# K's copy moved to VectorE, a third place for raw weight words, and a new planned order: pooled attention with a rational MLP on one Trainium2 core

## The chip, the cores and the metric

The kernel runs on one core of one Trainium2 chip. The metric is the device time of one execution in microseconds (us). The median of three runs before the change is 932.64 us.

## The reference

Pooled attention over 4 batches of 8 heads (1152 keys, 64 wide; pairs of queries are averaged, so 576 queries per head), then an MLP (512 to 2048 to 512) on 2304 tokens whose activation is a rational function.

```python
q_pool = q.reshape(B, H, S // 2, 2, D).mean(axis=3)
scores = 1.0 / np.sqrt(D) * np.matmul(q_pool, k.transpose(0, 1, 3, 2))
attn = np.exp(scores - np.max(scores, axis=-1, keepdims=True))
attn = attn / (np.sum(attn, axis=-1, keepdims=True) + 1e-09)
x = np.matmul(attn, v)          # then heads side by side: 2304 x 512
h = x @ w_in
P = a[0] + a[1] * h + a[2] * h**2 + a[3] * h**3
Q = 1.0 + np.abs(b[0]) * np.abs(h) + np.abs(b[1]) * h**2
out = (P / (Q + 1e-06)) @ w_out
```

## The kernel before

**Numbers.** Every factor of a product is split into a high and a low 16-bit part, so that f16 matmuls give nearly f32 results.

**Attention.** The work is cut into 16 preparations (one for each batch and each pair of heads) and 144 tiles of 128 queries. A preparation loads K, Q and V (SP's queue), takes their ranges (ACT, L608), splits them (ACT L662 to L669, DVE L675 to L684) and transposes K and Q by DMA (L689). A second copy of the upper 64 rows of K, `kb`, lies over a row of ones that was set once (`pr_kb`, L692, a DMA from SBUF to SBUF); with it the scores are computed again with the maximum subtracted in the product. For two head pairs of the last batch the operands are saved and read back later, and `kb` is made anew; that gives 18 copies in all. A tile is a chain: `at_fill` (PE, L720) makes scores in the PSUM tile `sc`, `at_max` (DVE, L727) reduces them, `at_turn` and `at_row` (PE L730, ACT L734) put the maximum into a row of Q, `at_fill2` (PE, L743 and L744, the second one with `kb`) makes scores with the maximum taken off in the PSUM tile `st`, `at_exp` (ACT, L751) takes the exponential and `at_split` (DVE, L759) scales its two halves. `at_pv` (PE, L773) multiplies with V. There is one `sc` and one `st`.

**Weights.** `w_in` and `w_out` arrive in 16 pieces each of 128 x 512 8-byte words into `NRAW=2` raw buffers (`w_load`, L458). Each piece is converted to f32 in the tile `wf` by ACT (`w_win`, L467), POOL (`w_low`, L471, in place) and DVE (`w_bits`, L475), and ACT takes its squares (`w_stat`, L480). When all 16 are there, 8 pairs of `w_hi` (ACT, L502) and `w_lo` (DVE, L506) write the 16-bit weights. `w_in` comes first, then four sums of its magnitudes that use the raw buffers again (L511), then `w_out` through the same buffers. `wf` has one buffer; before, each weight takes it as a tile of its own. When both weights are done, `w_close` gives the space to the MLP's tiles; everything of the MLP but `ch_rcp` (L874) and `ch_norm` waits for that (`late`).

**MLP.** 18 chunks of 128 tokens, each with 4 steps of two products (L915, and L986 to L988) with the activation on ACT, DVE and POOL between them. A chunk starts when its attention tiles are done: the first one needs the first two tiles of the fourth head pair of batch 0.

**Order.** Every engine runs its instructions in the order in which they are written out. That order is made on the host, before the launch, by `Plan`: each operation has an engine, a duration, a due time and the things that it reads and writes; `Plan.forward` schedules by rank, and some rounds back and forth keep the best. A DMA is costed as (issue, transfer, lead). `stirred` perturbs the best order with a random seed and keeps it where the planned end is earlier; before, the list of seeds, `stir`, is empty.

Of the kernel before, what the change touches and what calls it, by code (L numbers as in the profile page):

```python
# [29 lines left out]
    order0=[0, 4, 1, 5, 2, 6, 3, 7, 8], order1=[0, 4, 1, 5, 8, 2, 6, 3, 7], cv=5.63, p_head2=1.05, m0=8.0,  # L30
    stir=[],
    o=14.0, o_last=14.0, c0=2.0, mw=1.2, mf=1.2, ma=1.0, w0=60.0, w1=110.0, ws=2.5, wl=1.44,
# [237 lines left out]
def kernel(  # L270
# [54 lines left out]
    add = plan.add  # L325
    T_COPY, T_TR2 = 450, (625, 3050, 625)

    def cost(n_bytes):
        return (T_COPY, n_bytes / 360.0, T_COPY - 1)

# [115 lines left out]
    def w_open():  # L446
        st["stg_cm"] = tc.tile_pool(name="stg", bufs=1)
        st["stg"] = st["stg_cm"].__enter__()

    def w_load(n, i):  # L450

        t = st["stg"].tile([P, 512, 2], I32, tag="raw", name=f"raw_{n}{i}", bufs=NRAW)
        st["raw", n, i] = t
        if n == "wi":
            src = w_in.bitcast(I32)[i // 4 * P:(i // 4 + 1) * P, (i % 4) * 1024:(i % 4 + 1) * 1024]
        else:
            src = w_out.bitcast(I32)[i * P:(i + 1) * P, :]
        nc.sync.dma_start(out=t.rearrange("p f w -> p (f w)"), in_=src)  # L458
# [4 lines left out]
    def w_win(n, i):  # L463
        if i == 0:
            st["wf", n] = st["stg"].tile([P, 16, 512], F32, tag="wf", name=f"wf_{n}")
        u = st["raw", n, i][:, :, 1].bitcast(F32)
        nc.scalar.activation(out=st["wf", n][:, i, :], in_=u, func=AF.Prelu, scale=2.0 ** -111, alpha=-(2.0 ** 32))  # L467
# [223 lines left out]
    def pr_kb(j):  # L691
        nc.sync.dma_start(out=pr_new(j, "kb")[0:D], in_=pairs[j]["k"][0:D])  # L692

# [103 lines left out]
    def batches(c):  # L797
        return (c // 4,) if c < 4 * B else (2 * (c - 4 * B), 2 * (c - 4 * B) + 1)
# [225 lines left out]
    def prep(j, part):  # L1024
# [8 lines left out]
        if mode == "again":  # L1033
            if hp < 2:
                for i in (0, 1) if part == 0 else (2, 3, 4):
                    add("dma", cost(256 * op_cols(i)), at[6], lambda i=i: pr_again(j, i), r=[("kept", bb, hp, i)], w=[("set", o, i)], seq=["seqag"])
                if part == 0:
                    add("dma", (625, 820, 624), at[7], lambda: pr_kb(j), r=[("set", o, 1)], w=[("set", o, 5)])
            return
        if part == 1:  # L1040
            add("act", 1240, at[14], lambda: pr_hi(j, "v"), r=["vn", ("ss", j)], w=[("set", o, 2)])
            add("dve", 1500, at[15], lambda: pr_lo(j, "v"), r=["vn", ("ss", j), ("set", o, 2)], w=[("set", o, 3)])
            add("dve", 370, at[16], lambda: pr_v3(j), r=[("set", o, 2)], w=[("set", o, 4)])
            if mode == "first" and hp < 2:
                for i in range(5):
                    add("dma", cost(256 * op_cols(i)), at[17], lambda i=i: pr_save(j, i), r=[("set", o, i)], w=[("kept", bb, hp, i)], seq=["seqsv"])
            return
        add("dma", cost(128 * 4608), at[0], lambda: pr_load_k(j), w=["kn"])
        add("dma", (1400, 1640, 449), at[0], lambda: pr_load_q(j), w=["qn"])
        add("dma", cost(128 * 4608), at[1], lambda: pr_load_v(j), w=["vn"])  # L1050
        add("pool", 1500, at[6], lambda: pr_pool(j), w=["qn"])
        add("act", 1146, at[6], lambda: pr_stat(j, 0), r=["kn"], w=[("st", j), "spk"])
        add("act", 700, at[6], lambda: pr_stat(j, 1), r=["qn"], w=[("st", j), "spk"])
        add("act", 1146, at[6], lambda: pr_stat(j, 2), r=["vn"], w=[("st", j), "spk"])
        chain(at[7], half_exp(lambda: pairs[j]["st"]), w=[("st", j)])
# [6 lines left out]
        for i, w in enumerate(("k", "q")):  # L1062
            add("act", 1240, at[8 + 2 * i], lambda w=w: pr_hi(j, w), r=[w + "n", ("ss", j)], w=["sp" + w])
            add("dve", 820 if w == "q" else 1650, at[9 + 2 * i], lambda w=w: pr_lo(j, w), r=[w + "n", ("ss", j)], w=["sp" + w])
            add("dma", T_TR2, at[9 + 2 * i], lambda w=w: pr_tr(j, w), r=["sp" + w], w=[("set", o, 0 if w == "q" else 1)])
            if w == "k":
                add("dma", (625, 820, 624), at[10], lambda: pr_kb(j), r=[("set", o, 1)], w=[("set", o, 5)])

    def attend(t):
        j, slot = tiles[t]  # L1070
        o = j % 2
        s = time_of(t)
        jp = prep_of[j]
        E = ("E", t % NE)
        M = ("M", t % NM)
        wide = slot == 8
        add("pe", (650, 1100) if wide else (490, 960), s, lambda: at_fill(t), r=[("set", o, 0), ("set", o, 1)], w=["S"], seq=["seqS"], bank=B_S)
        add("dve", 1330, s + 0.6, lambda: at_max(t), r=["S"], w=[M], bank=B_S)
        add("pe", (60, 128), s + 2.1, lambda: at_turn(t), r=[M], w=["TURN"], seq=["seqM"], bank=B_TURN)
        add("act", 230, s + 2.3, lambda: at_row(t), r=["TURN", ("set", o, 0)], w=[("row", t)], bank=B_TURN)  # L1080
        add("pe", (1150, 2304) if wide else (1010, 2304), s + 2.7, lambda: at_fill2(t), r=[("row", t), ("set", o, 0), ("set", o, 1), ("set", o, 5)], w=["T"], seq=["seqT"], bank=B_T)
        add("act", 1300, s + 3.9, lambda: at_exp(t), r=["T", ("esc", jp)], w=[E], seq=["seqE"], bank=B_T)
        add("dve", 780, s + 5.3, lambda: at_split(t), w=[E], seq=["seql"])

    def product(g, host):
        j, bb, hp, slot, _ = at_rows(g)
        s = time_of(host) + PRM["pv"]
        V = ("PV", g % 2)
        jp = prep_of[j]
        x = ("x", slot, hp) if slot < 8 else ("x", slot, hp, bb % 2)  # L1090
        add("pe", (1600, 3000), s, lambda: at_pv(g), r=[("set", j % 2, i) for i in (2, 3, 4)] + [("E", t % NE) for t in groups[g]], w=[V], seq=["seqP"], bank=B_PV[g % 2])
        add("act", 370, s + PRM["pvx"], lambda: at_x(g), r=[V], w=[x], seq=["seqx"], bank=B_PV[g % 2])

    def weights(n, s0):
        for i in range(16):
            s = s0 + PRM["ws"] * i
            raw, wf = ("raw", i % NRAW), ("wf", i)
            add("dma", cost(128 * 4096), s, lambda i=i: w_load(n, i), w=[raw], seq=["raw"])
            add("act", 630, s + 4, lambda i=i: w_win(n, i), r=[raw], w=[wf], seq=["win"])
            add("pool", 830, s + 4, lambda i=i: w_low(n, i), w=[(*raw, "low")], r=[raw], seq=["low"])  # L1100
            add("dve", 800, s + 4, lambda i=i: w_bits(n, i), r=[raw, (*raw, "low")], w=[wf])
            add("act", 615, s + 6, lambda i=i: w_stat(n, i), r=[wf], w=[("wst", n, i)])
        s = s0 + 16 * PRM["ws"] + 2
# [4 lines left out]
        for i in range(8):  # L1108
            wf = [("wf", 2 * i), ("wf", 2 * i + 1)]
            add("act", 1141, s + PRM["wl"] * i, lambda i=i: w_hi(n, i), r=wf + [("sw", n)], w=[(n, 0, i)])  # L1110
            add("dve", 1330, s + PRM["wl"] * i, lambda i=i: w_lo(n, i), r=wf + [("sw", n), (n, 0, i)], w=[(n, 1, i)])
        s += 8 * PRM["wl"]
# [47 lines left out]
    def chunk(p):  # L1160
# [5 lines left out]
        svs = [("sv", bb, hp, 0) if c < 4 * B else ("sv", b_, hp, 1) for hp in range(NPAIR) for b_ in batches(c)]  # L1166
        add("dve", 420, u - 1.6, lambda: ch_rcp(c), r=xs + svs, w=["ri"])
        add("pool", 1400, u - 1.5, lambda: ch_norm(c), r=["ri"], w=xs)
        add("pool", 870, u, lambda: ch_hi(c), r=xs + [("cf", batches(c)), "late"], w=["xs"])
        add("dve", 900, u, lambda: ch_lo(c), r=xs, w=["xs"])  # L1170
        add("dma", (625, 900, 625), u, lambda: ch_tr(c), r=["xs"], w=[("X", p % XB)])
# [3 lines left out]
    def step(p, f):  # L1175
# [92 lines left out]
```

## Time and profile before

| | us |
|---|---|
| median of three runs | 932.64 (933.28, 927.57, 932.64) |
| profiled execution, its own time | 926.45 |
| its span, first to last instruction | 924.7 |
| PE, DVE, ACT, POOL busy | 809.6, 750.5, 620.5, 445.4 |
| mean granted TensorE clock | 0.954 |

Busy times are shares of the span. The granted clock is 1.0 at 2.4 GHz and 0.5 at 1.2 GHz; a stretch between has both levels in it. A wait is idle time of an engine, put down to what ended it. DVE is VectorE, ACT ScalarE, POOL GpSimd, PE TensorE, PEld its weight loads, SP the engine that issues all DMAs here.

### The profile page before, as it was taken

Reading aid. Unit: us, or ns where it says so; the run is one execution under the profiler, and the core shown is the slowest. Engines: PE = TensorE matmul, PEld = TensorE weight load, DVE = VectorE, ACT = ScalarE, POOL = GpSimd, SP = SyncE. Lnnn points to the kernel's source line nnn. Section 1 sums busy time; section 2 is a strip of 40 time slices with the busy share of each in tenths; the row PEclk is TensorE's granted clock in tenths of the full one; section 3 lists DMA queues with packets and bytes.
Section 4 is the critical chain, followed back from the end, with each engine's and each line's share of the span. In section 5 each row is a group of like instructions: output and inputs, shape, how many; then the busy total and the mean of one; then the engine's idle time right before and its main releaser. Section 6 shows DMA issues by size and latency. Waiting matters only on the chain.

```text
span 924.7 us, 27851 instructions
## 1 busy us (share of the span) xinstructions
PE 809.6 (88%) x12196; PEld 640.1 (69%) x12196; DVE 750.5 (81%) x1011; ACT 620.5 (67%) x937; POOL 445.4 (48%) x482
## 2 busy tenths in 40 slices
PE   0687587649999999899899999989999998999997
PEld 0475366537878887677678886777777777887773
DVE  5578887787988988769899888779989867977666
ACT  5579988765767767646856786666767746665452
POOL 3212235315755624458655552446855454445664
PEclk9988778958999999979999999989999999999999
DMA  7587376801600706612501234290917300521000
GB/s 217 160 210 199 80 189 214 222 24 44 135 25 1 155 2 154 144 34 48 119 13 26 44 112 91 73 245 14 236 32 155 70 20 14 164 68 25 24 13 23
DMA packets 121338, 88.80 MB, mean 96 GB/s; under 512 B 96768, under 2 KB 98816, under 8 KB 121216
## 3 DMA queue, kind: packets, MB, share of 16 engines
q1 hardware_dynamic: 121216, 87.02, 38.2%
q8 instruction: 95, 1.56, 0.7%
q14 instruction: 27, 0.22, 0.1%
HBM read 49.24 MB, written 8.87 MB: 63 GB/s over the span
## 4 chain that ended last, share of the span: by engine, by line
PE 54%; DVE 17%; ACT 11%; DMA 6%; issue 5%; POOL 4%; SPq 2%; POOLq 0%; DVEq 0%; ACTq 0%
PE ph_h L915 14%; PE st L743 6%; PE st L744 6%; PE sc L773 6%; PE st L773 5%; PE sc L720 5%; PE po L986 4%; PE po L988 4%; PE po L987 4%; ACT E L751 4%; DVE mt L727 3%; DVE E L759 2%; DVE t L941 2%; DVE g L965 2%; DVE t L937 2%
## 5 line engine op out<-in xcount | busy, mean ns | idle before, releaser
L751 ACT ACTIVATE E<-st,esc 128x1152 int32<-128x1152 f32 x144 | 188.6, 1310 | 68.3 <-PE st L730 45.7
L727 DVE TENSOR_REDUCE mt<-sc 128x1 f16<-128x1152 f32 x144 | 194.8, 1353 | 43.9 <-PE sc L720 32.5
L915 PEld LDWEIGHTS <-wi 128*128 128x128 f16 x3456 | 199.6, 99 | 24.2 <-DVE t L941 15.8
L915 PE MATMUL ph_h<-x,wi 128*128 128x128 f16 x3312 | 201.6, 221 | 10.5 <-DVE t L941 8.6
L743 PE MATMUL st<-q,k 128*128 128x128 f16 (+1 forms) x1440 | 179.4, 222 | 17.6 <-ACT q L734 12.2
L744 PE MATMUL st<-q,kb 65*128 65x128 f16 (+1 forms) x1440 | 179.8, 222 | 2.5 <-DMA kb<-k 2.5
L973 POOL TENSOR_TENSOR e<-t,e 128x512 f32<-128x512 f32 x72 | 111.4, 1547 | 141.3 <-DVE e L969 118.7
L744 PEld LDWEIGHTS <-kb 65*128 65x128 f16 x1440 | 137.8, 102 | 27.2 <-issue 21.0
L773 PEld LDWEIGHTS <-E 128*128 128x128 f16 (+1 forms) x4320 | 146.9, 103 | 11.5 <-issue 7.1
L743 PEld LDWEIGHTS <-k 128*128 128x128 f16 x1440 | 137.7, 102 | 17.2 <-issue 12.3
L759 DVE TENSOR_SCALAR E<-E 128x2304 f16<-128x2304 uint16 x144 | 126.8, 883 | 27.4 <-ACT E L751 27.2
L720 PE MATMUL sc<-k,q 128*128 128x384 f16 (+1 forms) x480 | 104.2, 353 | 41.2 <-DVE mt L727 28.6
L946 POOL TENSOR_SCALAR e<-A,b_abs 128x512 f32<-128x512 f32 x72 | 71.2, 989 | 82.5 <-ACT A L928 82.0
L988 PE MATMUL po<-wo,g 128*128 128x512 f16 x288 | 109.1, 379 | 1.6 <-DVE g L977 1.6
L986 PE MATMUL po<-wo,g 128*128 128x512 f16 x288 | 109.2, 379 | 0.0
L987 PE MATMUL po<-wo,g 128*128 128x512 f16 x288 | 109.1, 379 | 0.0
L950 POOL TENSOR_TENSOR e<-e,A 128x512 f32<-128x512 f32 x72 | 97.1, 1348 | 5.5
L720 PEld LDWEIGHTS <-q 128*128 128x128 f16 (+1 forms) x480 | 40.4, 105 | 73.7 <-issue 44.4
L928 ACT ACTIVATE A<-ph_h,cf 128x512 f32<-128x512 f32 x69 | 47.3, 685 | 58.5 <-PE ph_h L915 56.0
L954 ACT ACTIVATE A<-e,q_one 128x512 f32<-128x512 f32 x72 | 51.9, 720 | 48.3 <-POOL e L950 47.6
L977 DVE SCALAR_TENSOR_TENSOR g<-e,cf,A 128x512 f16<-128x512 f32 x72 | 64.9, 901 | 21.4 <-POOL e L973 21.3
L773 PE MATMUL sc<-v,E 128*128 128x65 f16 (+3 forms) x2160 | 77.3, 198 | 0.0
(124 smaller groups left out, 1175.7 us busy)
## 6 DMA issues: line engine op xcount, KB each, us to landing
kn<-in_k_dram SPq DMA_DIRECT2D x16, 576.0 KB, 4.5
vn<-in_v_dram SPq DMA_DIRECT2D x16, 576.0 KB, 5.2
qn<-in_q_dram SPq DMA_DIRECT2D x16, 512.0 KB, 4.9
raw_wi<-in_moe_w_in_dram SPq DMA_DIRECT2D x16, 512.0 KB, 4.8
raw_wo<-in_moe_w_out_dram SPq DMA_DIRECT2D x16, 512.0 KB, 4.5
kb<-k SPq DMA_DIRECT2D x18, 288.0 KB, 5.0
out_dram<-ob SPq DMA_DIRECT2D x16, 256.0 KB, 3.4
keep<-v SPq DMA_DIRECT2D x4, 292.5 KB, 5.7
```

The source lines that it names most:

```text
L720: nc.tensor.matmul(SC[ps, jj, 0:TH], d["q"][:, slot, ps], d["k"][:, h * KC + 3 * jj:h * KC + 3 * jj + 3, :].rearrange("p c m -> p (c m)"), ...
L727: nc.vector.tensor_reduce(mts[t % NM][:, D:D + 1], SC[:, :, 0:TH], AX.XY, ALU.max, negate=True)
L743: nc.tensor.matmul(o, d["k"][:, h * KC + c, :], d["q"][:, slot, qs], start=True, stop=False)
L744: nc.tensor.matmul(o, d["kb"][0:D + 1, h * KC + c, :], d["q"][0:D + 1, KC + slot, qs], start=False, stop=True)
L751: nc.scalar.activation(out=d["e"].rearrange("p (a c) -> p a c", a=3), in_=ST[:, :, 0:TH], func=AF.Exp, bias=esc[:, 1:2], scale=esc[:, 0:1],)
L759: nc.vector.tensor_scalar(e.bitcast(F16), e.bitcast(U16), 2.0 ** -6, None, ALU.mult)
L773: nc.tensor.matmul(pv[:, 0:w], e[:, c, qs, part], pairs[j][n_v][:, h * KC + c, :], start=(c == 0 and i == 0), stop=(c == KC - 1 and i == 2),)
L915: nc.tensor.matmul(mo[c, f]["p2"][:, i, :], wi[wl][:, kk, fs], x[:, xl * KD + kk, :], start=(n == 0), stop=(n == 3 * KD - 1))
L973: nc.gpsimd.tensor_tensor(w["e2"], w["t"], w["e2"], ALU.subtract)
L986: nc.tensor.matmul(po, g[0][:, e, :], wo[0][:, kk, :], start=(kk == 0), stop=False)
L987: nc.tensor.matmul(po, g[0][:, e, :], wo[1][:, kk, :], start=False, stop=False)
L988: nc.tensor.matmul(po, g[1][:, e, :], wo[0][:, kk, :], start=False, stop=(kk == KF - 1))
```

## The change

`pr_kb` becomes a copy by DVE. The one tile `wf` is taken once for both weights, and raw pieces 2, 5, 8 and 11 of each weight are loaded into its last two places, which are written last. Many durations that the planner uses are replaced; DMAs are costed at 270 in place of 360 bytes per ns, the transposes with 3300 in place of 3050 ns. `stir` gets 18 seeds, so the order of the whole program is another one.

```diff
-    stir=[],
+    stir=[5082, 5102, 5207, 5210, 5295, 5296, 5308, 5309, 5333, 5373, 5406, 5643, 5663, 5703, 5807, 5854, 5896, 5945],
...
-    T_COPY, T_TR2 = 450, (625, 3050, 625)
+    T_COPY, T_TR2 = 450, (625, 3300, 625)
...
-        return (T_COPY, n_bytes / 360.0, T_COPY - 1)
+        return (T_COPY, n_bytes / 270.0, T_COPY - 1)
...
+        st["wf", "wi"] = st["wf", "wo"] = st["stg"].tile([P, 16, 512], F32, tag="wf", name="wf")
+
+    IN_WF = (2, 5, 8, 11)
 
     def w_load(n, i):
 
-        t = st["stg"].tile([P, 512, 2], I32, tag="raw", name=f"raw_{n}{i}", bufs=NRAW)
+        if i in IN_WF:
+
+            t = st["wf", n][:, 14:16, :].bitcast(I32).rearrange("p a (f w) -> p (a f) w", w=2)
+        else:
+            t = st["stg"].tile([P, 512, 2], I32, tag="raw", name=f"raw_{n}{i}", bufs=NRAW)
...
     def pr_kb(j):
-        nc.sync.dma_start(out=pr_new(j, "kb")[0:D], in_=pairs[j]["k"][0:D])
+        nc.vector.tensor_copy(pr_new(j, "kb")[0:D], pairs[j]["k"][0:D])
...
-                    add("dma", (625, 820, 624), at[7], lambda: pr_kb(j), r=[("set", o, 1)], w=[("set", o, 5)])
+                    add("dve", 710, at[7], lambda: pr_kb(j), r=[("set", o, 1)], w=[("set", o, 5)])
...
-            add("dve", 1500, at[15], lambda: pr_lo(j, "v"), r=["vn", ("ss", j), ("set", o, 2)], w=[("set", o, 3)])
-            add("dve", 370, at[16], lambda: pr_v3(j), r=[("set", o, 2)], w=[("set", o, 4)])
+            add("dve", 1600, at[15], lambda: pr_lo(j, "v"), r=["vn", ("ss", j), ("set", o, 2)], w=[("set", o, 3)])
+            add("dve", 705, at[16], lambda: pr_v3(j), r=[("set", o, 2)], w=[("set", o, 4)])
...
-        add("dma", (1400, 1640, 449), at[0], lambda: pr_load_q(j), w=["qn"])
+        add("dma", (1400, 2200, 449), at[0], lambda: pr_load_q(j), w=["qn"])
...
-                add("dma", (625, 820, 624), at[10], lambda: pr_kb(j), r=[("set", o, 1)], w=[("set", o, 5)])
+                add("dve", 710, at[10], lambda: pr_kb(j), r=[("set", o, 1)], w=[("set", o, 5)])
...
-        add("dve", 780, s + 5.3, lambda: at_split(t), w=[E], seq=["seql"])
+        add("dve", 870, s + 5.3, lambda: at_split(t), w=[E], seq=["seql"])
...
-            raw, wf = ("raw", i % NRAW), ("wf", i)
+            home = sum(j not in IN_WF for j in range(i)) % NRAW
+            raw, wf = ("wf", 14) if i in IN_WF else ("raw", home), ("wf", min(i, 14))
...
-        add("pool", 1400, u + PRM["m_rem"], lambda: mo_rem(c, f), r=[T], w=[E2])
-        add("dve", 800, u + PRM["m_glo"], lambda: mo_glo(c, f), r=[A], w=[G, E2, T])
+        add("pool", 1530, u + PRM["m_rem"], lambda: mo_rem(c, f), r=[T], w=[E2])
+        add("dve", 900, u + PRM["m_glo"], lambda: mo_glo(c, f), r=[A], w=[G, E2, T])
```

Some seventeen further durations of ACT, DVE and POOL operations change in the same way, each by at most 109 ns but `ch_norm`'s (1400 to 1250).

## Rows read from the trace of the kernel before

**Rows 1.** The page: span, busy time of two engines, granted clock in 40 slices.
```profile
span 924.7 us, 27851 instructions
PE 809.6 (88%) x12196; PEld 640.1 (69%) x12196; DVE 750.5 (81%) x1011; ACT 620.5 (67%) x937; POOL 445.4 (48%) x482
PEclk9988778958999999979999999989999999999999
```

**Rows 2.** Stretches: length, PE, PEld, DVE, ACT, POOL busy (instructions), clock, DMA share, GB/s.
```profile
50.00:100.00 50.00, 37.10 (x612) 32.06 (x610) 40.13 (x50) 41.03 (x72) 12.99 (x16) 0.83 0.83 213
...
125.00:150.00 25.00, 17.78 (x281) 14.41 (x282) 18.78 (x31) 18.96 (x38) 10.54 (x16) 0.86 0.94 239
150.00:175.00 25.00, 18.87 (x298) 14.89 (x298) 19.26 (x25) 20.94 (x38) 12.76 (x18) 0.86 0.90 240
175.00:206.00 31.00, 15.21 (x191) 11.67 (x191) 24.90 (x35) 23.59 (x40) 5.41 (x6) 0.70 0.27 79
...
225.00:450.00 225.00, 215.54 (x3390) 172.78 (x3388) 192.70 (x257) 156.55 (x229) 125.56 (x135) 0.98 0.38 83
450.00:600.00 150.00, 147.80 (x2344) 117.01 (x2342) 128.82 (x169) 101.36 (x149) 75.46 (x79) 1.00 0.24 58
600.00:750.00 150.00, 143.64 (x2184) 114.10 (x2181) 133.00 (x176) 101.93 (x152) 84.54 (x78) 0.98 0.50 118
750.00:842.00 92.00, 88.22 (x1478) 74.12 (x1476) 73.25 (x99) 57.61 (x85) 44.69 (x58) 1.00 0.25 68
842.00:925.00 83.00, 75.89 (x861) 52.38 (x857) 54.67 (x70) 36.29 (x56) 49.33 (x41) 1.00 0.08 20
```

**Rows 3.** Timeline of DVE, 160 to 225 us: start, duration, instruction, idle before it.
```profile
181.94 0.16 DVE L874 SCALAR_TENSOR_TENSOR ri<-xf,sv 128x8 f32<-128x8 f32 x1
...
196.57 9.65 DVE L506 SCALAR_TENSOR_TENSOR wo<-wf_wo,sw_wo,wo 128x1024 f16<-128x1024 f32 x8
...
207.42 0.74 DVE L888 SCALAR_TENSOR_TENSOR xs<-xf,cf,xs 128x512 f16<-128x512 f32 x1
```

**Rows 4.** The tile `raw_wo`: ns min/median/max, first and last start in us.
```profile
L458 SPq DMA_DIRECT2D raw_wo<-in_moe_w_out_dram x16: 327/335/715, 125.9 to 180.8; - x16
L475 DVE SCALAR_TENSOR_TENSOR wf_wo<-wf_wo,raw_wo x16: 669/693/703, 131.8 to 186.5; 128x512 int32<-128x512 int32 x16
...
DMA to landing us min/median/max: 3.3/4.5/6.3
```

**Rows 5.** Waits of the whole span: who waited for whom, us in total, times, longest.
```profile
PE sc L720 <- DVE mt L727: 28.6, 22, 10.3
POOL raw_wo L471 <- DMA raw_wo<-in_moe_w_out_dram: 20.1, 9, 4.7
...
PE ph_h L915 <- DVE t L941: 8.6, 13, 1.2
```

**Rows 6.** The tile `kb`: forms, idle time before them, time to landing.
```profile
L692 SPq DMA_DIRECT2D kb<-k x18: 476/532/701, 25.0 to 811.0; - x18
L434 DVE MEMSET kb<- x2: 1978/1978/1978, 2.8 to 5.2; 1x2304 f16 x2
...
DMA to landing us min/median/max: 3.2/5.0/9.8
```

**Rows 7.** Timeline, 25 to 45 us: DVE's first maximum, PE's first use of `kb`.
```profile
25.06 1.36 DVE L727 TENSOR_REDUCE mt<-sc 128x1 f16<-128x1152 f32 x1 [4.31 <-PE sc L720]
...
32.92 0.29 PE L744 MATMUL st<-q,kb 65*128 65x128 f16 x1 [2.52 <-DMA kb<-k]
```

**Rows 8.** Groups by line: `at_split` (busy us, mean ns, idle before); then its ns min/median/max.
```profile
L759 DVE TENSOR_SCALAR E<-E 128x2304 f16<-128x2304 uint16 x144 | 126.8, 883 | 27.4 <-ACT E L751 27.2
...
L759 DVE TENSOR_SCALAR E<-E x144: 728/753/1836, 37.9 to 841.7; 128x2304 f16<-128x2304 uint16 x144
```

**Rows 9.** The tile `spk`: K's transposes, and their time to landing.
```profile
L689 SPq DMA_TRANSPOSE k<-spk x16: 2690/3706/5166, 16.3 to 731.4; - x16
...
DMA to landing us min/median/max: 4.6/6.1/7.7
```

**Rows 10.** The chain that ended last, in order of time: start, us, what.
```profile
599.44 2.68 DMA out_dram<-ob
...
606.71 4.67 DMA x<-xs
...
664.28 6.92 DMA vn<-in_v_dram
```

More of the change, by code (lines that the diff above doesn't have):

```diff
@@ L463, in w_win @@
     def w_win(n, i):
-        if i == 0:
-            st["wf", n] = st["stg"].tile([P, 16, 512], F32, tag="wf", name=f"wf_{n}")
         u = st["raw", n, i][:, :, 1].bitcast(F32)
@@ L1048, in prep @@
         add("dma", cost(128 * 4608), at[0], lambda: pr_load_k(j), w=["kn"])
-        add("dma", (1400, 1640, 449), at[0], lambda: pr_load_q(j), w=["qn"])
+        add("dma", (1400, 2200, 449), at[0], lambda: pr_load_q(j), w=["qn"])
         add("dma", cost(128 * 4608), at[1], lambda: pr_load_v(j), w=["vn"])
         add("pool", 1500, at[6], lambda: pr_pool(j), w=["qn"])
-        add("act", 1146, at[6], lambda: pr_stat(j, 0), r=["kn"], w=[("st", j), "spk"])
-        add("act", 700, at[6], lambda: pr_stat(j, 1), r=["qn"], w=[("st", j), "spk"])
-        add("act", 1146, at[6], lambda: pr_stat(j, 2), r=["vn"], w=[("st", j), "spk"])
+        add("act", 1255, at[6], lambda: pr_stat(j, 0), r=["kn"], w=[("st", j), "spk"])
+        add("act", 773, at[6], lambda: pr_stat(j, 1), r=["qn"], w=[("st", j), "spk"])
+        add("act", 1255, at[6], lambda: pr_stat(j, 2), r=["vn"], w=[("st", j), "spk"])
         chain(at[7], half_exp(lambda: pairs[j]["st"]), w=[("st", j)])
@@ L1063, in prep @@
             add("act", 1240, at[8 + 2 * i], lambda w=w: pr_hi(j, w), r=[w + "n", ("ss", j)], w=["sp" + w])
-            add("dve", 820 if w == "q" else 1650, at[9 + 2 * i], lambda w=w: pr_lo(j, w), r=[w + "n", ("ss", j)], w=["sp" + w])
+            add("dve", 850 if w == "q" else 1560, at[9 + 2 * i], lambda w=w: pr_lo(j, w), r=[w + "n", ("ss", j)], w=["sp" + w])
             add("dma", T_TR2, at[9 + 2 * i], lambda w=w: pr_tr(j, w), r=["sp" + w], w=[("set", o, 0 if w == "q" else 1)])
             if w == "k":
-                add("dma", (625, 820, 624), at[10], lambda: pr_kb(j), r=[("set", o, 1)], w=[("set", o, 5)])
+                add("dve", 710, at[10], lambda: pr_kb(j), r=[("set", o, 1)], w=[("set", o, 5)])
     def attend(t):
@@ L1077, in attend @@
         add("pe", (650, 1100) if wide else (490, 960), s, lambda: at_fill(t), r=[("set", o, 0), ("set", o, 1)], w=["S"], seq=["seqS"], bank=B_S)
-        add("dve", 1330, s + 0.6, lambda: at_max(t), r=["S"], w=[M], bank=B_S)
+        add("dve", 1353, s + 0.6, lambda: at_max(t), r=["S"], w=[M], bank=B_S)
         add("pe", (60, 128), s + 2.1, lambda: at_turn(t), r=[M], w=["TURN"], seq=["seqM"], bank=B_TURN)
-        add("act", 230, s + 2.3, lambda: at_row(t), r=["TURN", ("set", o, 0)], w=[("row", t)], bank=B_TURN)
+        add("act", 268, s + 2.3, lambda: at_row(t), r=["TURN", ("set", o, 0)], w=[("row", t)], bank=B_TURN)
         add("pe", (1150, 2304) if wide else (1010, 2304), s + 2.7, lambda: at_fill2(t), r=[("row", t), ("set", o, 0), ("set", o, 1), ("set", o, 5)], w=["T"], seq=["seqT"], bank=B_T)
         add("act", 1300, s + 3.9, lambda: at_exp(t), r=["T", ("esc", jp)], w=[E], seq=["seqE"], bank=B_T)
-        add("dve", 780, s + 5.3, lambda: at_split(t), w=[E], seq=["seql"])
+        add("dve", 870, s + 5.3, lambda: at_split(t), w=[E], seq=["seql"])
     def product(g, host):
@@ L1091, in product @@
         add("pe", (1600, 3000), s, lambda: at_pv(g), r=[("set", j % 2, i) for i in (2, 3, 4)] + [("E", t % NE) for t in groups[g]], w=[V], seq=["seqP"], bank=B_PV[g % 2])
-        add("act", 370, s + PRM["pvx"], lambda: at_x(g), r=[V], w=[x], seq=["seqx"], bank=B_PV[g % 2])
+        add("act", 276, s + PRM["pvx"], lambda: at_x(g), r=[V], w=[x], seq=["seqx"], bank=B_PV[g % 2])
     def weights(n, s0):
@@ L1096, in weights @@
             s = s0 + PRM["ws"] * i
-            raw, wf = ("raw", i % NRAW), ("wf", i)
+            home = sum(j not in IN_WF for j in range(i)) % NRAW
+            raw, wf = ("wf", 14) if i in IN_WF else ("raw", home), ("wf", min(i, 14))
             add("dma", cost(128 * 4096), s, lambda i=i: w_load(n, i), w=[raw], seq=["raw"])
[L1099 to L1102, printed above, removed]
+            add("act", 670, s + 4, lambda i=i: w_win(n, i), r=[raw], w=[wf], seq=["win"])
+            add("pool", 830, s + 4, lambda i=i: w_low(n, i), w=[("low", n, i)], r=[raw], seq=["low"])
+            add("dve", 715, s + 4, lambda i=i: w_bits(n, i), r=[raw, ("low", n, i)] if raw != wf else [("low", n, i)], w=[wf])
+            add("act", 715, s + 6, lambda i=i: w_stat(n, i), r=[wf], w=[("wst", n, i)])
         s = s0 + 16 * PRM["ws"] + 2
@@ L1108, in weights @@
         for i in range(8):
-            wf = [("wf", 2 * i), ("wf", 2 * i + 1)]
+            wf = [("wf", min(2 * i, 14)), ("wf", min(2 * i + 1, 14))]
             add("act", 1141, s + PRM["wl"] * i, lambda i=i: w_hi(n, i), r=wf + [("sw", n)], w=[(n, 0, i)])
-            add("dve", 1330, s + PRM["wl"] * i, lambda i=i: w_lo(n, i), r=wf + [("sw", n), (n, 0, i)], w=[(n, 1, i)])
+            add("dve", 1280, s + PRM["wl"] * i, lambda i=i: w_lo(n, i), r=wf + [("sw", n), (n, 0, i)], w=[(n, 1, i)])
         s += 8 * PRM["wl"]
@@ L1166, in chunk @@
         svs = [("sv", bb, hp, 0) if c < 4 * B else ("sv", b_, hp, 1) for hp in range(NPAIR) for b_ in batches(c)]
[L1167 to L1170, printed above, removed]
+        add("dve", 515, u - 1.6, lambda: ch_rcp(c), r=xs + svs, w=["ri"])
+        add("pool", 1250, u - 1.5, lambda: ch_norm(c), r=["ri"], w=xs)
+        add("pool", 950, u, lambda: ch_hi(c), r=xs + [("cf", batches(c)), "late"], w=["xs"])
+        add("dve", 850, u, lambda: ch_lo(c), r=xs, w=["xs"])
         add("dma", (625, 900, 625), u, lambda: ch_tr(c), r=["xs"], w=[("X", p % XB)])
@@ L1194, in step @@
         add("act", 620, u + PRM["m_ln"], lambda: mo_r(c, f), w=[A])
-        add("dve", 750, u + PRM["m_ghi"], lambda: mo_ghi(c, f), r=[T, A], w=[G], seq=["seqG"])
-        add("dve", 770, u + PRM["m_d1"], lambda: mo_d1(c, f), r=[G], w=[E2])
-        add("pool", 1400, u + PRM["m_rem"], lambda: mo_rem(c, f), r=[T], w=[E2])
-        add("dve", 800, u + PRM["m_glo"], lambda: mo_glo(c, f), r=[A], w=[G, E2, T])
+        add("dve", 820, u + PRM["m_ghi"], lambda: mo_ghi(c, f), r=[T, A], w=[G], seq=["seqG"])
+        add("dve", 805, u + PRM["m_d1"], lambda: mo_d1(c, f), r=[G], w=[E2])
+        add("pool", 1530, u + PRM["m_rem"], lambda: mo_rem(c, f), r=[T], w=[E2])
+        add("dve", 900, u + PRM["m_glo"], lambda: mo_glo(c, f), r=[A], w=[G, E2, T])
         po = "po_t" if last else "po"
```

## The prediction, made before the change was run

> **What bounds the kernel now.** I read the page first, for who is busy and where the clock falls: PE is busy 809.6 of 924.7 us, and the slices of the granted clock show that the low ones lie nearly all in the first quarter [rows 1]. So there are two stages, and I then read a table of stretches, busy time beside clock. A PE busy time at a clock below 1.0 is worth less, so I multiply the two. From 225 to 842 us that gives 215.5 x 0.98 + 147.8 + 143.6 x 0.98 + 88.2 = 588 of 617 us, 95%: this stage is bound by PE. From 150 to 175 us it is 18.9 x 0.86 = 16.2 of 25, 65%, and from 175 to 206 us 15.2 x 0.70 = 10.6 of 31, 34% [rows 2]. The head is where PE's time is lost.
>
> What holds the head is seen on DVE's timeline. `ri` (L874), the first step of the first chunk, runs at 181.9 us: its attention is ready then. But its next DVE step, `xs` (L888), comes at 207.4 us, right behind the eight `w_lo` of `w_out` that end at 206.2 us [rows 3]. So the MLP waits 24 us for the weights alone. The weights in turn are paced by their buffers: the 16 loads of `w_out` are issued from 125.9 to 180.8 us, 15 steps of 3.66 us, which is 7.3 us for a turn of one of the two buffers; 4.5 us of that is a load from issue to landing (median) [rows 4]. POOL, the first to touch a piece, waited 20.1 us for such loads [rows 5].
>
> **The change part by part.** The sum is made against the profiled execution's own 926.45 us. The three timed runs lie at 927.57 to 933.28, median 932.64, so the profile stands 6.2 us below the median.
>
> *The first copy of K.* PE stood 2.5 us for the DMA of `kb` before its first L744 at 32.9 us [rows 7]. A DVE copy would be there sooner: DVE stood idle 4.3 us before its first maximum at 25.1 us [rows 7], when Q's and K's transposes were landing, and that hides it. Gain 2.5 us; without that cover the copy's own 0.75 us is off it.
>
> *The other 17 copies.* The other copies' DMAs show no PE wait, though they took 3.2 to 9.8 us to land [rows 6]; removing them gains nothing on the path. They go to DVE. The nearest row is `at_split`, 2304 16-bit values per partition like the copy: median 753 ns [rows 8]. Upper bound: the memset of one row of 2304 took 1978 ns [rows 6]; lower bound: the least split, 728. I take 753 ns, as size and type are the same: 17 x 0.753 = 12.8 us of DVE (12.4 to 33.6). DVE has 617 - (192.7 + 128.8 + 133.0 + 73.3) = 89 us idle from 225 to 842 us [rows 2], which hides most. How much of a DVE microsecond reaches PE: PE waited for L727 and L941 28.6 + 8.6 = 37 us [rows 5] beside DVE's 750 us busy [rows 1], a share of 0.05. So 0.6 us, taken as +1; with no cover it is +12.8.
>
> *The lock.* `at_split` is stretched from 753 to 1836 ns at worst, and its mean is 883 [rows 8]: 130 ns more on average, 18 x 0.13 = 2.3 us on DVE, of which the share above is nothing. The Trainium skill (SBUF — State Buffer, section "SBUF: two separate sides") says that a DVE operation that uses two ports and a GpSimd operation take the shared ports in turns, each for its whole length, which speaks against moving a copy to DVE. The spread of `at_split` agrees with that; by this rule each copy also holds POOL off, 18 x 0.753 = 13.6 us at most, and the sum would be up to that much higher. POOL is busy 445 of 925 us [rows 1], so I let it hide.
>
> *The third place for raw words.* With pieces 2, 5, 8 and 11 in the free end of `wf`, three loads are in flight up to piece 12: the pace there can fall from 7.3 / 2 = 3.66 to 7.3 / 3 = 2.44 us, 11 x 1.22 = 13.4 us for `w_out` [rows 4]. Nothing is gained if ACT and DVE are the next limit: they are busy 20.9 and 19.3 of 25 us there [rows 2]. I take two thirds, 9 us, since a fifth of both is idle, and another 9 for `w_in`, whose earlier end moves all of `w_out` up. Their sum, 18, is within the 24 us after which the first chunk's attention is the limit. What it is worth: in these microseconds PE worked at 34% to 65% and would work at 95% instead, so each is worth 0.3 to 0.6; at 0.5 it is 9 us (0 to 12). The copy of the piece-2 load into `wf` must wait until the last pair of `w_in` has been read, but `w_out`'s loads start behind that anyway; this costs nothing.
>
> *The new order.* The old plan believed in 360 bytes per ns. Where the DMA engines are nearly full, 239 GB/s at a share of 0.94 and 213 at 0.83, the rate is 213 / 0.83 = 257 and 239 / 0.94 = 254 [rows 2], so 270 is close to the truth and the old plan dated transfers too early. No row prices another order. Bounds: PE's idle time from 225 us on is 700 - 671 = 29 us [rows 2], of which about 7 in the last 83 us is the end of the last chunk; 22 is the most to be had, and an order can as well lose. The nearest rows are the transfers on the chain late in the program, three of 2.7, 4.7 and 6.9 us, 14 us [rows 10]. I take half, 7 us.
>
> Also moved: SP no longer issues 18 DMAs of 0.53 us [rows 6], and what stood behind them in its queue (Q's and V's loads, output) goes that much earlier; no wait of PE hangs on it.
>
> Sum: -2.5 + 1 - 9 - 7 = -17.5, so 926.45 - 17.5 = 909 us beside the profile. The timed runs scatter up to 6 us above their profile, so I forecast 912 us for their median, half-way.
>
> **The rivals.**
> *A, the copy waits on DVE (slower).* DVE runs in order. The copy can start only when K's transpose has landed, 4.6 to 7.7 us after its issue, median 6.1 [rows 9]; the plan (625 + 650 + 3300 + 960 ns from the code and the diff) counts on 5.5. Where the copy comes next on DVE it stands there for the difference, 0.6 us at the median, 2.2 at worst, and the maximum of a tile, a split or an MLP step behind it stands too; PE then waits for L727, as it does already 22 times [rows 5]. 16 transposes x 0.6 to 2.2 is 10 to 35 us. At 17.5 / 16 = 1.1 us per copy the gain is gone; at 1.7 the kernel is slower by 1%. At the worst row: 912 + 35 = 947. For it: DVE is full in parts of the main stage. Against: a planner that knows the date puts other work ahead. Chance that the waits are over 1.1 us a copy, so 929 to 947 us: 0.15.
>
> *B, no change.* ACT and DVE, 77% to 84% busy in the head [rows 2], do not get the pieces done sooner however early they land, or w_out's third place is not free in time; and the new order loses in one place what it gains in another. Then only -2.5 + 1 is left: 925 beside the profile, about 930. The lock's 13.6 us on the path would end at 912 + 13.6 = 926, in this case too (0.04 of it). Chance 0.23 in all.
>
> *C, much faster.* The 12 us of the head are had in full, and the order gains the 22 us of the main stage: -2.5 + 1 - 12 - 22 = -35.5, 891 beside the profile, 894 in the runs. For it: both the durations and the seeds bear on all of the program. Against: PE's waits there are many and short. Chance 0.14.
>
> **How the numbers follow.** The forecast has 0.48; its own range is 902 to 924, from the head at 4 to 12 and the order at 0 to 14. About 1% is what a measurement of this kernel tells from no change, 923 to 942 us. Faster by more: the forecast, C, and none of the rest, 0.48 + 0.14 = 0.62. Within: B and A's smaller third, 0.23 + 0.05 = 0.28. Slower: the rest of A, 0.10. For eight in ten the range runs from C's value to A's smaller third: 894 to 935, which leaves out half of C and most of A, under 0.2.
>
> **What would show it.** Right: no wait of PE for `kb` at the first L744; loads of `w_out` some 2.5 us apart up to piece 12; the last `w_lo` before 195 us, and the first L915 before 200; PE idle after 225 us below 29 us. Wrong: the weights' loads come early but `w_lo` still ends at 206; or DVE shows idle time before the copies put down to K's transpose, several us in all, with longer waits of PE for L727 behind. If the head is as short as I say and the time is not, the order has lost in the main stage, and PE's idle time there is over 40 us.

## The result, and the profile after

The changed kernel takes 901.5 us (median of four runs, 899.12 to 902.86) against 932.52 before: a ratio of 0.9675, 95% interval 0.9636 to 0.9715. The profiled execution took 901.19 us against 926.45, 25.3 us less. That lies in the range given (894 to 935) and just below the forecast's own one (902 to 924).

The page of the changed kernel first: span, busy times, the granted clock in 40 slices, as in [rows 1].

```profile
span 899.4 us, 27832 instructions
PE 802.4 (89%) x12196; PEld 641.2 (71%) x12196; DVE 760.1 (85%) x1029; ACT 618.7 (69%) x937; POOL 447.2 (50%) x482
PEclk9968988799999999999999999799999999999999
```

DVE is busy 9.6 us more for 18 more instructions. The slices of the granted clock show 9, but for one of them, from the ninth slice (180 us) on; in [rows 1] they do so, but for two, from the eleventh (231 us). DVE's timeline shows what comes just before that (start, duration, instruction; most lines of the changed kernel have numbers higher by five, so L506 is now L511 and L915 is L920):

```profile
165.94 7.21 DVE L511 SCALAR_TENSOR_TENSOR wo<-wf,sw_wo,wo 128x1024 f16<-128x1024 f32 x5
173.08 0.15 DVE L879 SCALAR_TENSOR_TENSOR ri<-xf,sv 128x8 f32<-128x8 f32 x1
...
173.39 4.41 DVE L511 SCALAR_TENSOR_TENSOR wo<-wf,sw_wo,wo 128x1024 f16<-128x1024 f32 x3
...
178.99 0.73 DVE L893 SCALAR_TENSOR_TENSOR xs<-xf,cf,xs 128x512 f16<-128x512 f32 x1
```

In [rows 3] `ri` stood at 181.9 us and `xs` at 207.4, 25 us apart, since the last `w_lo` ended at 206.2. Now the last `w_lo` ends at 177.8, `ri` falls between the `w_lo`, and `xs` follows at 179.0. The first MLP product (L920) comes at 183.1 us in place of 211.4.

So I cut both traces at the first MLP product. The stretch table for before, then after (length, PE, PEld, DVE, ACT, POOL busy with instructions, clock, DMA share, GB/s); the first line of each pair is the head, the second the work behind it without its last 60 us:

```profile
0.00:211.40 211.40, 125.69 (x1759) 97.74 (x1760) 158.62 (x232) 159.24 (x260) 60.97 (x89) 0.85 0.63 167
211.40:864.70 653.30, 630.74 (x9913) 507.58 (x9913) 552.50 (x732) 435.29 (x639) 348.34 (x365) 0.98 0.34 80
```
```profile
0.00:183.10 183.10, 111.01 (x1672) 90.28 (x1673) 150.91 (x223) 155.43 (x251) 58.87 (x87) 0.86 0.66 185
183.10:839.40 656.30, 637.87 (x9982) 515.14 (x9983) 570.80 (x760) 438.46 (x649) 353.76 (x367) 0.98 0.31 74
```

The same cut, with the exponentials (one for each attention tile) alone: before, then after.

```profile
0.00:211.40 211.40, 41.92 (x32) 0.85 0.63 167
```
```profile
0.00:183.10 183.10, 40.97 (x32) 0.86 0.66 185
```

The reader sees three things. The head is 28.3 us shorter. It holds 32 exponentials both times, as the same tiles of attention come before the first chunk. And what comes behind is 716.3 us in place of 713.3. The whole gain is in the head.

For the rest of the text I split the time behind the head into PE's work at the full clock and what is lost beside it. The work is the number of matmuls of each line times the length of one as the chain shows it at 2.4 GHz (24 of L920 in 1.34 us, 54 of L778 in 1.63 us, 3 of L725 in 0.49 us, L991 to L993 0.21 us each, 0.213 in the sums; L735, L748 and L749 are taken like L920). One attention tile in nine has matmuls of 64 columns in L748 and L749, which start 0.03 us apart and are counted here like those of 128; this makes the work some 12 us too large and the loss as much too small, in all kernels alike (13 such tiles lie behind the head before and after). So only differences between kernels are read from this split, and each comes from one profiled execution. Behind the head this gives 668.1 us of work and 45.2 lost before, 673.7 and 42.6 after. So 25.3 = 28.3 (head) - 5.6 (work that had been done in the head and now comes behind it) + 2.6 (less lost).

### The profile page after: what moved, and what is told of

Its sections match the earlier page's. It is cut to its first block, busy times and chain, and to the rows that moved or that the text cites. A ratio compares the mean times of both kernels' runs of the same rounds, so it can differ in the third digit from the quotient of the medians.

```text
span 899.4 us, 27832 instructions
## 1 busy us (share of the span) xinstructions
PE 802.4 (89%) x12196; PEld 641.2 (71%) x12196; DVE 760.1 (85%) x1029; ACT 618.7 (69%) x937; POOL 447.2 (50%) x482
## 4 chain that ended last, share of the span: by engine, by line
PE 63%; DVE 14%; ACT 5%; issue 3%; POOL 2%; DMA 2%; DVEq 0%; ACTq 0%; POOLq 0%
PE ph_h L920 17%; PE sc L778 6%; PE st L748 6%; PE st L749 6%; PE st L778 5%; PE sc L725 5%; PE po L991 5%; PE po L993 5%; PE po L992 5%; DVE mt L732 3%; ACT E L756 3%; DVE E L764 1%; DVE g L970 1%; DVE g L982 1%; DVE wo L511 1%
## 5 line engine op out<-in xcount | busy, mean ns | idle before, releaser
L732 DVE TENSOR_REDUCE mt<-sc 128x1 f16<-128x1152 f32 x144 | 194.7, 1352 | 35.8 <-PE sc L725 20.8
L920 PEld LDWEIGHTS <-wi 128*128 128x128 f16 x3456 | 201.8, 99 | 17.0 <-DVE t L946 8.8
L920 PE MATMUL ph_h<-x,wi 128*128 128x128 f16 x3312 | 204.3, 222 | 5.5 <-DVE t L946 4.9
L748 PE MATMUL st<-q,k 128*128 128x128 f16 (+1 forms) x1440 | 178.0, 221 | 26.4 <-ACT q L739 22.3
L749 PE MATMUL st<-q,kb 65*128 65x128 f16 (+1 forms) x1440 | 178.5, 221 | 0.0
L749 PEld LDWEIGHTS <-kb 65*128 65x128 f16 x1440 | 137.2, 102 | 35.9 <-issue 31.5
L778 PEld LDWEIGHTS <-E 128*128 128x128 f16 (+1 forms) x4320 | 147.8, 103 | 13.3 <-issue 7.9
L978 POOL TENSOR_TENSOR e<-t,e 128x512 f32<-128x512 f32 x72 | 105.9, 1470 | 103.0 <-DVE e L974 92.2
L748 PEld LDWEIGHTS <-k 128*128 128x128 f16 x1440 | 137.3, 102 | 19.7 <-issue 13.3
L951 POOL TENSOR_SCALAR e<-A,b_abs 128x512 f32<-128x512 f32 x72 | 73.3, 1018 | 132.2 <-ACT A L933 132.0
L764 DVE TENSOR_SCALAR E<-E 128x2304 f16<-128x2304 uint16 x144 | 123.7, 863 | 14.3 <-ACT E L756 13.9
L725 PE MATMUL sc<-k,q 128*128 128x384 f16 (+1 forms) x480 | 100.6, 345 | 29.7 <-DVE mt L732 15.5
L993 PE MATMUL po<-wo,g 128*128 128x512 f16 x288 | 109.1, 379 | 1.6 <-DVE g L982 1.6
L991 PE MATMUL po<-wo,g 128*128 128x512 f16 x288 | 109.3, 379 | 0.8 <-ACT ob L997 0.8
L778 PE MATMUL sc<-v,E 128*128 128x65 f16 (+3 forms) x2160 | 79.2, 200 | 0.0
L778 PE MATMUL st<-v,E 128*128 128x65 f16 (+3 forms) x2160 | 73.7, 195 | 2.3 <-ACT E L756 1.5
L725 PEld LDWEIGHTS <-q 128*128 128x128 f16 (+1 forms) x480 | 38.9, 104 | 51.0 <-issue 20.8
```

The costliest lines, as they stand in the source:

```text
L725: nc.tensor.matmul(SC[ps, jj, 0:TH], d["q"][:, slot, ps], d["k"][:, h * KC + 3 * jj:h * KC + 3 * jj + 3, :].rearrange("p c m -> p (c m)"), ...
L732: nc.vector.tensor_reduce(mts[t % NM][:, D:D + 1], SC[:, :, 0:TH], AX.XY, ALU.max, negate=True)
L748: nc.tensor.matmul(o, d["k"][:, h * KC + c, :], d["q"][:, slot, qs], start=True, stop=False)
L749: nc.tensor.matmul(o, d["kb"][0:D + 1, h * KC + c, :], d["q"][0:D + 1, KC + slot, qs], start=False, stop=True)
L764: nc.vector.tensor_scalar(e.bitcast(F16), e.bitcast(U16), 2.0 ** -6, None, ALU.mult)
L778: nc.tensor.matmul(pv[:, 0:w], e[:, c, qs, part], pairs[j][n_v][:, h * KC + c, :], start=(c == 0 and i == 0), stop=(c == KC - 1 and i == 2),)
```

## The experiments

Theory H was mine: the third place for raw words makes the head short. Rival O: the new order does it, and the place is not needed. Rival K: K's copy on DVE is itself a main part. After the first four runs a theory S was added, that the time is the head plus some 712 us whatever is changed, with a rival P, that the place pays only with the new durations and seeds. In runs whose name begins with "held" the written order of the changed kernel is kept and one thing is exchanged in it; in the others the planner makes a new order for the parts named.

**The third place taken away, order held.**

```diff
-        if i in IN_WF:
+        if i in ():
```

> The changed kernel with its order kept as it is; only the raw pieces 2, 5, 8 and 11 go into the two raw buffers too, so the third place is not used. Theory H (the third place made the head short): loads wait for their buffers again, 3.66 us apart in place of some 2.5, w_out's conversion ends 13 to 28 us later than at 158 us, the first MLP product comes at 195 to 211 in place of 183 us, and the time goes to 913 to 930 us. Theory O (the new order made it short, the place is not needed): the first product stays within 4 us of 183 and the time within 5 us of 901.5.

Measured: 914.5 us, ratio 0.9836 (0.9765 to 0.9907). The head, and the loads of `w_out` here and then in the changed kernel, whose other four go to `wf` (ns min/median/max, first and last start):

```profile
0.00:199.00 199.00, 116.96 (x1671) 94.34 (x1672) 151.45 (x223) 156.61 (x251) 57.43 (x87) 0.86 0.61 170
```
```profile
L465 SPq DMA_DIRECT2D raw_wo<-in_moe_w_out_dram x16: 327/328/455, 111.4 to 166.2; - x16
...
L465 SPq DMA_DIRECT2D raw_wo<-in_moe_w_out_dram x12: 327/328/860, 102.2 to 150.4; - x12
```

The loads are 54.8 / 15 = 3.65 us apart again, as in [rows 4]; with the place they are issued from 102.2 to 150.4, 3.21 us apart. The head is 15.9 us longer and the span 15.8: what the head gains here arrives whole, since the order behind it is the same. By the medians it is 13.0 us (914.5 and 901.5), and the intervals of the two ratios do not meet. Theory H holds for 16 of the 28 us. Rival O is left with the other 12, as the held order without the place has a head of 199.0 and not of 211.4; the copy on DVE is in these 12, and the next run prices it.

**K's copy by DMA again, order held; and for the later preparations alone.**

```diff
-        nc.vector.tensor_copy(pr_new(j, "kb")[0:D], pairs[j]["k"][0:D])
+        nc.sync.dma_start(out=pr_new(j, "kb")[0:D], in_=pairs[j]["k"][0:D])
```

> The changed kernel with its order kept; only K's copy is a DMA on SP's queue again, where the order has it. Theory H (the copies' DMAs were hidden but for the first): 2.5 us more at the first L749 and at most 1 us at each other preparation, 904 to 912 us. Rival K (the copy on DVE is itself a main part of the gain, because an order can count on 0.75 us where the DMA took 3 to 10): PE waits for kb in most of the 18 places, 2 us or more each, and the time is 925 us or above.

Measured: 899.2 us, ratio 0.9677 (0.9640 to 0.9714); the changed kernel has 0.9675 (0.9636 to 0.9715). The copy on DVE gains nothing that can be told. The work behind the head, and the DMA's time to landing:

```profile
185.10:836.40 651.30, 633.90 (x9977) 511.32 (x9976) 562.59 (x745) 438.24 (x649) 350.02 (x367) 0.98 0.34 80
```
```profile
DMA to landing us min/median/max: 3.1/4.1/5.8
```

The head is 2.0 us longer (185.1), the work behind it loses 37.3 us in place of 42.6, and DVE is busy 8 us less there. No wait of PE is put down to `kb`: the first L749 starts at 31.4 us, 1.5 us later than with the copy (29.9) but 1.5 us earlier than before (32.9, L744 in [rows 7]), and what PE waited for just ahead of it was ACT (L739, 1.2 us). So in this order the DMA of the first `kb` is no longer what holds PE. Rival K falls, and so does the forecast of this run, 904 us or more. That the copy gains in the head and costs behind it is what the two profiles say; so I mixed them.

```diff
+        copy = nc.vector.tensor_copy if j < 4 else nc.sync.dma_start
+        copy(out=pr_new(j, "kb")[0:D], in_=pairs[j]["k"][0:D])
```

> The changed kernel with its order kept; K's copy on DVE for the first four preparations (the head) and by DMA for all later ones. If the copy gains 2 us in the head and costs 5 us of a full DVE behind it, as the two profiles of the held order say: first product at 183 us as in the changed kernel, the rest 711 us as with the DMA, in all 2 to 4 us below the run with all copies by DMA: 895 to 898 us. If that difference is only the scatter of single profiles: 899 to 902 us.

Measured: 898.6 us, ratio 0.9673 (0.9643 to 0.9702), the head 185.5 us, behind it 710.9; the time lies between the two that were expected. As far as single profiles tell, the 2 us in the head do not come back with the copy on DVE, so they are not the copy's; the 5 us behind the head stay, but the times of the three kernels can't be told apart.

**The seeds.**

```diff
-    stir=[5082, 5102, 5207, 5210, 5295, 5296, 5308, 5309, 5333, 5373, 5406, 5643, 5663, 5703, 5807, 5854, 5896, 5945],
+    stir=[],
```

> The changed kernel with an empty list of seeds: the same parts and durations, the order without the 18 perturbations. Theory H: the seeds are worth a few us in the main stage, 903 to 910 us, the first MLP product within 8 us of 183. Theory O: they carry most of the gain, 918 us or more, mostly from a longer head.

```diff
-    stir=[5082, ..., 5945],
+    stir=list(range(100, 160)),
```

> The changed kernel with 60 other seeds (100 to 159) in place of its 18. If any search of the order helps as the given seeds do: head 178 to 190 us and 897 to 905 us. If the 18 seeds were a lucky choice, or a search by the planned end does not carry to the chip: 905 to 915 us, like or worse than no seeds (906.3).

Measured: without seeds 906.3 us, ratio 0.9750 (0.9706 to 0.9794), head 192.2 us; with 60 other seeds 903.8 us, 0.9749 (0.9678 to 0.9819), head 189.2 us. Without the seeds the head is 9.1 us longer, but 37.3 us are lost behind it and not 42.6. The medians differ by 0.75% for the given seeds, and the intervals overlap; what the seeds gave lies in the head and not in the main stage, where theory H had looked for it. Other seeds were worth nothing that can be told by the ratio (0.9749 and 0.9750), though 903.8 us is a time that the first of the two expectations allowed.

**Single parts, each with an order planned for it.** First the durations alone: the changed kernel with its place, its seeds and its copy taken out.

```diff
-    IN_WF = (2, 5, 8, 11)
+    IN_WF = ()
...
-                add("dve", 710, at[10], lambda: pr_kb(j), r=[("set", o, 1)], w=[("set", o, 5)])
+                add("dma", (625, 1090, 624), at[10], lambda: pr_kb(j), r=[("set", o, 1)], w=[("set", o, 5)])
...
```

> The kernel before with the new durations alone (and wf taken once for both weights): K's copy stays a DMA, costed (625, 1090, 624) by the new 270 bytes per ns, no third place, no seeds. Theory H: the head is still paced by two raw buffers, first MLP product after 200 us, 922 to 930 us. Theory O: the true DMA durations alone make the head short, 905 to 915 us.

The place alone, in the kernel before:

```diff
+    IN_WF = (2, 5, 8, 11)
...
+        if i in IN_WF:
+            t = st["wf", n][:, 14:16, :].bitcast(I32).rearrange("p a (f w) -> p (a f) w", w=2)
...
```

> The kernel before with the third place for raw words alone (and wf taken once); old durations, K's copy by DMA, no seeds, a new order planned for it. Theory S (the time is the length of the head, up to the first MLP product, plus some 712 us, whatever is changed): the third place makes the head shorter by 10 to 20 us and the time by as much, 910 to 920 us. Rival P (the place pays only with the new durations and seeds): first product after 205 us, 923 us or more.

Durations and copy, which is the changed kernel without seeds and without the place; then with 60 seeds:

```diff
-    IN_WF = (2, 5, 8, 11)
+    IN_WF = ()
...
```

> New durations and K's copy on DVE, without the third place and without seeds. Theory S: against the run without seeds alone (head 192 us, 906 us) the head is 12 to 20 us longer and the time 916 to 925 us; against the run with the durations alone (head 215 us, 924 us) K's copy on DVE gives 0 to 6 us. Rival K: the copy gives 10 us or more here, 913 us or less.

> The same 60 seeds, new durations and K's copy on DVE, but no third place. Theory S (two raw buffers hold the head, an order can't make up for it): head 200 us or more, 912 to 924 us, 8 to 20 us above the run with the same seeds and the place. Theory O (the search makes up for the missing place): within 6 us of that run.

| parts | us | ratio (interval) | head | work behind | lost behind |
|---|---|---|---|---|---|
| none (before) | 932.5 | 1 | 211.4 | 668.1 | 45.2 |
| durations | 923.6 | 0.9939 (0.9913 to 0.9966) | 214.6 | 666.0 | 41.9 |
| durations, copy | 923.9 | 0.9940 (0.9905 to 0.9975) | 211.6 | 667.8 | 43.8 |
| durations, copy, 60 seeds | 918.5 | 0.9897 (0.9835 to 0.9959) | 208.0 | 666.7 | 37.4 |
| place, old durations | 927.7 | 0.9985 (0.9964 to 1.0006) | 200.5 | 675.0 | 49.0 |
| durations, copy, place | 906.3 | 0.9750 (0.9706 to 0.9794) | 192.2 | 671.4 | 37.3 |
| durations, copy, place, 60 seeds | 903.8 | 0.9749 (0.9678 to 0.9819) | 189.2 | 672.9 | 48.1 |
| all, its 18 seeds | 901.5 | 0.9675 (0.9636 to 0.9715) | 183.1 | 673.7 | 42.6 |

The median of the kernel before is that of its own comparison; beside the other runs it was 928.7 to 929.8 us, so lines are compared by their ratios. Heads, work and losses are those of one profiled execution each (that of the 60 seeds with the place was 912 us, its slowest of four). The durations give 0.6%, and the copy beside them nothing that can be told (0.9940 and 0.9939). Without the place no order had a head below 199 us; theory S is right there, rival O falls for the rest, and the place is worth 1.9% with the new durations and no seeds, 1.5% with the 60 seeds. But theory S, as "the head plus 712 us", falls with the place under the old durations:

```profile
0.00:200.50 200.50, 126.47 (x1653) 101.25 (x1654) 148.87 (x219) 154.56 (x249) 56.17 (x87) 0.81 0.66 176
...
200.50:864.50 664.00, 639.77 (x10019) 515.57 (x10020) 570.64 (x747) 442.10 (x652) 357.44 (x368) 0.98 0.33 79
```
```profile
0.00:200.50 200.50, 39.46 (x31) 0.81 0.66 176
```

Its head is 10.9 us shorter than before, and nothing of it arrives: the head holds 31 exponentials in place of 32, and 106 matmuls fewer, which leaves 6.9 us more of work behind it, and 3.8 us more are lost there. So rival P holds for this pair in the time, if not in the head: the place paid only with the new durations. Each side of the pair is one planned order, so how general this is stays open.

**A fourth place, and the copy planned as a DMA.**

```diff
-    IN_WF = (2, 5, 8, 11)
+    IN_WF = {2: 14, 3: 12, 6: 14, 7: 12, 10: 14, 11: 12}
...
```

> The changed kernel without seeds, and with a fourth place: of raw pieces 0 to 11 of each weight two in four go to the free places 12 and 14 of wf. Theory S with the places still the limit: loads come closer together again, the head is 5 to 12 us shorter than the 192 us of the run without seeds, and the time 894 to 901 us. If with three places ACT and DVE have become the limit: head within 3 us of 192 and 903 to 909 us.

```diff
-                add("dve", 710, at[10], lambda: pr_kb(j), r=[("set", o, 1)], w=[("set", o, 5)])
+                add("dma", (625, 1090, 624), at[10], lambda: pr_kb(j), r=[("set", o, 1)], w=[("set", o, 5)])
...
```

> The same 60 seeds with the third place, K's copy by DMA and planned as such (625, 1090, 624). If the copy's place doesn't matter: within 6 us of the run with the same seeds and the copy on DVE; the work behind the head loses 3 to 6 us less, as in the held order, and the first copies may cost the head 2 to 3 us. If an order needs the short copy: 8 us or more above it.

Measured: the fourth place, without seeds, 916.3 us, 0.9869 (0.9817 to 0.9920), head 199.1 us; three places had 192.2. The second, 60 seeds and the copy by DMA, 902.9 us, 0.9714 (0.9656 to 0.9772), not to be told from the copy on DVE with the same seeds (0.9749). Its head is 193.9 us and its profile loses only 32.8 us behind it, but this profile is the fastest of its four runs (898.0 us) and the other's the slowest, so the two losses can't be compared. Both forecasts for the fourth place fall. Its order differs everywhere, so the run does not say whether the place or the order is at fault. Its loads of `w_out` are issued from 115.1 to 169.0 us, 3.59 us apart as with two buffers, so the fourth place did not bring them closer together. The head moved by 9 us between three orders of the same parts too (183.1, 189.2, 192.2).

**Less ACT work in the head, order held.**

```diff
+        if i:
+            return
         place = wi[0][:, i // 4, (i % 4) * 512:(i % 4 + 1) * 512] if n == "wi" else wo[0][:, i, :]
...
```

> The changed kernel with its order kept; of the 16 squares of each weight only the first is taken (the scale comes from that piece alone), 30 x 0.8 = 24 us of ACT less in the head. If ACT is what now holds the head (155 of 183 us busy): the head is 10 us shorter or more, 883 to 892 us. If it is the loads, DVE or the first chunk's attention: 3 us at most, 898 to 903 us.

Measured: 898.6 us, 0.9684 (0.9628 to 0.9739).

```profile
0.00:184.00 184.00, 112.90 (x1671) 91.83 (x1671) 150.54 (x223) 136.69 (x191) 59.02 (x87) 0.85 0.65 184
```

ACT is busy 136.7 us in place of 155.4 and the head is 184.0 us long. In this order ACT is not what holds the head. Which of the loads, DVE and the tiles' chain does was not tried; on the chain that ended last, half of the time from 160 to 183 us is `w_lo` of `w_out` on DVE (49.8%).

No version beats the changed kernel clearly; the held order with K's copy by DMA is as fast.

## Why the prediction was right, step by step

- **What bounds it.** Right: the head was held by the weights. The last `w_lo` came before 195 us (177.8) and the first MLP product before 200 (183.1), as the prediction asked. PE's idle time from 225 us on is below 29 us: the stretches from 225 to 900 us hold 650.3 us of PE's busy time, so 24.7 us.
- **The third place.** It was put at 18 us of earlier weights, 9 for each. The held order shows 16: without the place the last square of `w_in` starts 9.5 us later (72.9 and 63.4 us) and that of `w_out` 15.9 us later (173.5 and 157.6), of which `w_out`'s own conversion has 6.4. Size and split were about right, the mechanism was not quite: up to piece 12 the loads of `w_out` are 3.24 us apart (102.2 to 141.1), and not the 2.5 that the prediction asked for as a sign. Without the seeds they are 2.28 us apart (121.1 to 148.4), with a longer head. The squares of `w_in` before, in the held order without the place, and after (ns min/median/max, first and last start):

```profile
L480 ACT ACTIVATE wi<-wf_wi x16: 612/630/632, 11.7 to 99.2; 128x512 f16<-128x512 f32 x16
...
L485 ACT ACTIVATE wi<-wf x16: 612/617/632, 12.8 to 72.9; 128x512 f16<-128x512 f32 x16
...
L485 ACT ACTIVATE wi<-wf x16: 613/625/631, 12.4 to 63.4; 128x512 f16<-128x512 f32 x16
```

- **The order.** This term was sought in the wrong stage. It was put at 7 us, all in the main stage, from transfers on the chain there [rows 10]. Behind the head 2.6 us less are lost. In the head, where the prediction gave it nothing, it gave 12.4 us (211.4 to 199.0, the held order without the place). The last square of `w_in`, which started at 99.2 us before, starts at 72.9 us there: the order brings the loads of `w_in` forward (issued from 3.6 to 63.1 us and not to 87.3), which the prediction had booked to the place alone. In sum, order and copies brought the profiled span from 924.7 to 915.2 us, 9.5 us, where the forecast had 8.5 for them. That the two are close is luck, as the gain came from another stage; by the medians (ratio 0.9836) it is some 15 us.
- **What a microsecond of head is worth.** This is the mis-sized term. It was put at 0.5, from the rate of PE's work there, so 18 us of earlier weights were to give 9; in the held order 15.9 us gave 15.8, a price of 1.0 (13.0 us by the medians). Over the whole change it is 22.7 of 28.3, 0.80. The prediction took it that PE's work in the time cut off the head would have to be done behind it. But the head holds 32 exponentials both times, and in the held pair as many matmuls (1671 and 1672), so that work was not pushed back but done in less time. With the place under the old durations the price was below the forecast's: 10.9 us of head gave 4.0 us before the losses, 0.37, and nothing after them. So the price hangs on whether the order keeps the tiles in the head.
- **The first copy of K.** The first L749 comes at 29.9 us in place of 32.9 [rows 7], with no wait for `kb` before it. But the copy is at most half of these 3.0 us, as the held order with the DMA starts it at 31.4 us without a wait for `kb` either; and it does not reach the end, as the time with the DMA can't be told from it. The forecast counted 2.5 us from PE's one wait; what took them up was not traced.
- **The other copies.** Put at +1 us. The copy took a median of 744 ns, beside the 753 assumed [rows 8]. Behind the head the loss falls from 42.6 to 37.3 us without them, +5 at most, in single profiles; in the runs it can't be seen.
- **Rival A, the copy waiting on DVE.** It did not come. DVE never sat idle before a copy in the changed kernel (first the times of the copies, then their busy time, mean and idle time before them), and PE's waits for the maximum (L727, now L732) fell from 28.6 us [rows 5] to 15.5:

```profile
L697 DVE COPY kb<-k x18: 737/744/1958, 21.1 to 789.5; 64x2304 f16<-64x2304 f16 x18
...
L697 DVE COPY kb<-k 64x2304 f16<-64x2304 f16 x18 | 14.8, 824 | 0.0
```

Rival B fell with the head, and rival C came half-way: the head gave more than its 12 us, the main stage almost nothing of its 22.
- **The lock.** One copy was stretched from 744 to 1958 ns: it started at 621.3 us, while POOL's L598 ran from 620.7 to 622.6. The other 17 took 930 ns at most. The Trainium skill (SBUF — State Buffer, section "SBUF: two separate sides") describes such a block between DVE and GpSimd on their shared ports, and this row agrees with it. No run here shows that it cost time: POOL's busy time rose from 445.4 to 447.2 us only.

The sum of the forecast, -17.5, and the measured -25.3 differ by the head: 9 were given to it and 22.7 came, while the main stage was given 7 and gave 2.6, and K's copies were given a gain of 1.5 and gave none that shows. In the timed runs the forecast was 912 us and 901.5 came: the range held, but of the two terms that made the gain one was priced too low (9 us for 13 to 16) and the other was expected in the wrong stage.

## What to carry to other kernels

Where a pipeline has a filling stage whose end is set by a dependency, cut the trace at the first instruction behind it and count the work on both sides: a shorter stage is worth its full length only as far as the same work is still done in it. A wait is not yet the gain of removing it; here PE's wait of 2.5 us for `kb` was gone in the new order with the copy and with the DMA, and the times of the two can't be told apart. And a free place for loads and the order that uses it belong together: the place alone brought nothing that can be told (0.15%), the durations alone 0.6%, both with the copy 2.5%.

## What the runs showed beyond the expectation

The DMA that copies K from SBUF to SBUF, which took 3.2 to 9.8 us to land in the old order [rows 6], took 3.1 to 5.8 in the new one (the held order with the copies by DMA), with the same 18 copies; with the 60 seeds it took 3.0 to 10.4. The long ones come and go with the order. A copy of 64 partitions by 2304 16-bit values takes DVE 744 ns, about as long as the split of 128 partitions by 2304 (753), another operation on twice the partitions. And three orders made from the same parts differ by up to 9 us in the head and by 11 us in what is lost behind it (37.3, 42.6, 48.1), though the profile with the largest loss is 8 us slower than the median of its runs.
